# One row order for every chunk of a pointwise convolution, and its first load on a second queue

## Chip, cores and metric

The kernel runs on one core of a Trainium2 chip. The metric is device time in microseconds (us) of one execution; the profiled span is about 1.7 us shorter than that time. A run told with a profile has one execution in the trace, and its other executions only as times; a traced execution is called a look.

## The reference, cut to what matters

With `k = 1` the depthwise part is a scale of each of the 384 channels, and the rest is a matmul by the 384 x 384 pointwise weights:

```python
out = x * dw[0, 0]                                # x: 1 x 384 x 384 x 384, bf16
return jnp.einsum('bhwc,cd->bhwd', out, pw)       # pw: 384 x 384
```

That is 147456 rows of 768 bytes in, and as many out.

## The kernel before

The scale is folded into the weights at the start: the row `dw` becomes a selection matrix `sel_w`, and 18 small matmuls (L216) spread and scale the weights into `w_r`. Then come 288 supertiles of 512 rows. For each, VectorE transposes x into `T`, TensorE does 48 matmuls (L166) of 32 rows by 384 columns, four at a time in the four row groups of the array, and ScalarE casts the result from PSUM into `O`. Supertiles are loaded and stored in chunks of `L`: 1, 1, 2, 2, 4 at the start, then tens, then 6, 4, 3, 2, 1, 1, 1. The parts that the change touches:

```python
LONG = 3
...
def load_x(t):
    g, i, off, first, L = chunks[t]
    dst = Xs[g % NR][:, 4 * off : 4 * (off + L), :]
    rows = xf[512 * first : 512 * (first + L), :]
    if first + LONG < NS:                     # all chunks but the last three
        src = rows.rearrange("(p s) c -> p (s c)", p=P)
        dst = dst.rearrange("p s c -> p (s c)")
    else:                                     # the last three, one supertile each
        src = rows.rearrange("(a k q) c -> q a k c", k=4, q=4)
    ...
    nc.sync.dma_start(dst, src).then_inc(s_x[g % NR][i], 16)

def store(t):
    ...
    if first + LONG < NS:
        dst = rows.rearrange("(q p j) d -> p q (j d)", q=4, p=P)
        src = src.rearrange("p (q e) -> p q e", q=4)
    else:
        dst = rows.rearrange("(m q) d -> m (q d)", q=4)
    ...                                       # wait for the casts of the chunk
    nc.sync.dma_start(dst, src).then_inc(s_o[g % NR], 16)

nc.scalar.dma_start(dw_row[:], ...)           # depthwise row, ScalarE's queue
nc.sync.dma_start(pw_n[:], ...)               # weights, SyncE's queue
# then load_x(0), load_x(1), ... on SyncE's queue
```

For a chunk of one supertile the two branches are mirror images. "By quadrant" loads 128 pieces of 3 KB and stores 512 pieces of 768 bytes. "The other row order" loads 512 pieces of 768 bytes and stores 128 pieces of 3 KB. Load and store have to use the same one, or rows come out permuted.

## Time and profile before

| | before |
|---|---|
| time, median of 3 (range) | 575.43 us (575.23 to 576.05) |
| span of the profiled run | 573.7 us |
| TensorE, main matmuls | 561.8 us |
| head: start of the main loop | 7.18 us |
| last cast ends | 569.97 us |
| last store: issue to landing | 2.3 us |

TensorE is busy for 99% of the span. Only what stands before the first main matmul (the head) and what follows the last one (the tail) can change the time. The lines that carry this are in the prediction. One more, because the experiments turn on it, is ScalarE's timeline at the start of the main loop (start, length, engine and line, work, idle time before it and its releaser):

```profile
9.36 1.44 ACT L307 CAST O<-ps 128x1536 bf16<-128x1536 f32 x1 [0.92 <-PE ps L166]
```

This is the cast of the first supertile. It starts 9.36 - 7.18 = 2.18 us after the main loop does.

### The profile page before, as it was taken

The numbers are of one execution on the slowest core, as the hardware profiler recorded it, in microseconds if no ns is written. First come the engines' busy times: TensorE is split into PE (matmuls) and PEld (weight loads), VectorE is DVE, ScalarE is ACT, GpSimd is POOL, SyncE is SP. The second block draws the span as 40 slices with busy tenths as digits, with TensorE's granted clock in tenths as the row PEclk, the third lists the DMA queues.
The fourth block names the chain that finished last, engine by engine and source line by source line (L and its number), as shares of the span: only waits on it lengthen the run. The fifth ranks groups of instructions, "written<-read, shape, count | busy, mean of one in ns | idle before, by whom it ended". The sixth has DMA issues, their size and how long they took to land.

```text
span 573.7 us, 29706 instructions
## 1 busy us (share of the span) xinstructions
PE 567.3 (99%) x13869; PEld 414.9 (72%) x13869; DVE 509.3 (89%) x583; ACT 418.8 (73%) x296; POOL 0.9 (0%) x8
## 2 busy tenths in 40 slices
PE   8999999999999999999999999999999999999996
PEld 5777777777777777777777777777777777777774
DVE  6899999999999999999999999999999999999994
ACT  6777777777777777777777777777777777777775
POOL 0000000000000000000000000000000000000000
PEclk9999999999999999999999999999999999999999
DMA  8999999999999999999999999999999999994996
GB/s 324 432 409 417 430 397 430 444 424 422 399 408 416 384 397 436 398 383 395 432 398 384 395 429 390 393 401 429 402 385 419 401 390 397 425 394 149 402 408 251
DMA packets 25912, 226.88 MB, mean 395 GB/s; under 512 B 1197, under 2 KB 5678, under 8 KB 22062
## 3 DMA queue, kind: packets, MB, share of 16 engines
q1 hardware_dynamic: 25900, 226.79, 98.0%
q14 instruction: 9, 0.07, 0.0%
q8 instruction: 1, 0.02, 0.0%
q10 hardware_dynamic: 2, 0.00, 0.0%
HBM read 113.54 MB, written 113.25 MB: 395 GB/s over the span
## 4 chain that ended last, share of the span: by engine, by line
PE 98%; DMA 1%; ACT 0%; DVE 0%; issue 0%; SPq 0%
PE ps L166 97%; DMA pw_n<-in_pw_dram 1%; PE ps L216 1%; DMA out_dram<-O 0%; ACT O L307 0%; DVE O L304 0%; SPq L337 0%; SPq L100 0%
## 5 line engine op out<-in xcount | busy, mean ns | idle before, releaser
L166 PE MATMUL ps<-w_r,T 32*128 32x384 bf16 x13824 | 561.8, 321 | 0.1
L258 DVE STREAM_TRANSPOSE T<-X 128x384 uint32<-128x384 uint32 x576 | 506.2, 882 | 54.0 <-DMA X<-in_x_dram 2.4
L307 ACT CAST O<-ps 128x1536 bf16<-128x1536 f32 x288 | 413.5, 1436 | 147.9 <-PE ps L166 147.9
L166 PEld LDWEIGHTS ps<-w_r,T 32*128 32x128 bf16 x13824 | 412.9, 93 | 149.2 <-issue 0.7
L271 ACT CAST w_r<-ps 128x768 bf16<-128x768 f32 x5 | 3.7, 805 | 1.7 <-PE ps L216 1.6
L183 PE MATMUL ps<-zero 32*128 32x384 bf16 x24 | 2.6, 494 | 1.4 <-POOL zero L232 1.4
L304 DVE CAST O<-ps 128x768 bf16<-128x768 f32 x1 | 1.0, 958 | 3.0 <-DMA out_dram<-O 3.0
L216 PE MATMUL ps<-pw_n,sel_w 64*128 64x384 bf16 x18 | 3.0, 510 | 0.1
L183 PEld LDWEIGHTS ps<-zero 32*128 32x128 bf16 x24 | 0.7, 100 | 2.6 <-issue 2.6
L216 PEld LDWEIGHTS ps<-pw_n,sel_w 64*128 64x128 bf16 x18 | 1.2, 138 | 1.6 <-issue 1.2
L244 ACT ACT_TABLE_LOAD x1 | 1.3, 1283 | 1.5 <-SPq L100 1.5
L276 DVE TENSOR_REDUCE sel<-eye 128x64 f32<-128x128 bf16 x1 | 0.3, 290 | 1.8 <-POOL eye L234 1.8
L271 DVE CAST w_r<-ps 128x768 bf16<-128x768 f32 x1 | 1.0, 956 | 1.0 <-PE ps L216 1.0
L286 DVE TENSOR_SCALAR sel_w<-sel,dw_f 128x256 bf16<-128x256 f32 x3 | 0.9, 348 | 0.0
L283 DVE COPY dw_f<-ps 128x3 f32<-128x3 f32 x1 | 0.2, 161 | 0.8 <-PE ps L198 0.8
L198 PEld LDWEIGHTS ps<-ones,dw_row 1*128 1x128 bf16 x3 | 0.2, 98 | 0.2 <-issue 0.2
L244 ACT COPY warm<-warm 128x1 f32<-128x1 f32 x2 | 0.3, 188 | 0.0
L234 POOL TENSOR_SCALAR_AFFINE_SELECT eye<-ones 128x128 bf16<-128x128 bf16 x1 | 0.3, 292 | 0.1
L232 POOL MEMSET zero<- 128x192 uint32 x1 | 0.3, 258 | 0.0
L198 PE MATMUL ps<-ones,dw_row 1*128 1x1 bf16 x3 | 0.2, 159 | 0.0
L233 POOL MEMSET ones<- 128x128 bf16 x1 | 0.2, 204 | 0.0
L231 POOL MEMSET warm<- 128x3 f32 x1 | 0.1, 101 | 0.5 <-SPq L100 0.5
(4 smaller groups left out, 0.4 us busy)
## 6 DMA issues: line engine op xcount, KB each, us to landing
X<-in_x_dram SPq DMA_DIRECT2D x26, 3840.0 KB, 21.5
out_dram<-O SPq DMA_DIRECT2D x26, 3840.0 KB, 27.5
X<-in_x_dram SPq DMA_DIRECT2D x2, 1536.0 KB, 17.4
out_dram<-O SPq DMA_DIRECT2D x2, 1536.0 KB, 13.7
X<-in_x_dram SPq DMA_DIRECT2D x3, 768.0 KB, 8.8
out_dram<-O SPq DMA_DIRECT2D x3, 768.0 KB, 8.9
X<-in_x_dram SPq DMA_DIRECT2D x1, 2304.0 KB, 18.9
out_dram<-O SPq DMA_DIRECT2D x1, 2304.0 KB, 12.1
```

The costliest lines, as they stand in the source:

```text
L166: mm = nc.tensor.matmul(PS[s][:, q, :D], lhsT=Ts[s][32 * q : 32 * q + 32, b, par::2], rhs=w_r[32 * q : 32 * q + 32, b, par, :], start=(b, ...
L183: nc.tensor.matmul(PS[0][:, i, :D], lhsT=zero[32 * i : 32 * i + 32, 0:P], rhs=zero[32 * i : 32 * i + 32, :], start=True, stop=True, tile_p ...
L198: mm = nc.tensor.matmul(PS[1][:, 0, D + k : D + k + 1], lhsT=dw_row[:, P * k : P * k + P], rhs=ones[0:1, 0:1], start=True, stop=True,)
L216: mm = nc.tensor.matmul(PS[(k + 1) % 2][:, 2 * r + v, :D], lhsT=sel_w[64 * v : 64 * v + 64, k, r, :, :].rearrange("p q w -> p (q w)"), rhs ...
L232: nc.gpsimd.memset(zero[:].bitcast(U32), 0).then_inc(s_zero)
L234: nc.gpsimd.affine_select(out=eye[:], in_=ones[:], pattern=[[-1, P]], compare_op=mybir.AluOpType.is_equal, fill=0.0, base=0, channel_multi ...
L244: c = nc.scalar.copy(warm[:, s + 1 : s + 2], warm[:, 0:1])
L258: ins = nc.vector.transpose(out=Tw[:, 3 * h : 3 * h + 3], in_=Xw[:, :, j, 96 * h : 96 * h + 96].rearrange("p k (b w) -> p b k w", w=32),)
L271: o = nc.vector.tensor_copy(out, in_) if e == 0 else nc.scalar.copy(out, in_)
L286: nc.vector.tensor_scalar_mul(sel_w[:, k], sel[:].unsqueeze(2).to_broadcast([P, 2, 4, 32]), dw_f[:, k : k + 1]).then_inc(s_sw)
L304: e = nc.vector.tensor_copy(Ov[:, nq:4, j, :], PS[s][:, nq:4, :D])
L307: a = nc.scalar.copy(Ov[:, 0:nq, j, :], PS[s][:, 0:nq, :D])
```

## The change

Intent: one row order for all chunks, so that the special case goes away, and the first chunk of x is issued on ScalarE's queue, in parallel with the weights on SyncE's. The diff, without blank lines and context:

```diff
-LONG = 3
-        def load_x(t):
+        def load_x(t, eng=nc.sync):
-            if first + LONG < NS:
-                src = rows.rearrange("(p s) c -> p (s c)", p=P)
-                dst = dst.rearrange("p s c -> p (s c)")
-            else:
-                src = rows.rearrange("(a k q) c -> q a k c", k=4, q=4)
+            src = rows.rearrange("(p s) c -> p (s c)", p=P)
+            dst = dst.rearrange("p s c -> p (s c)")
-            nc.sync.dma_start(dst, src).then_inc(s_x[g % NR][i], 16)
+            eng.dma_start(dst, src).then_inc(s_x[g % NR][i], 16)
...
-            if first + LONG < NS:
-                dst = rows.rearrange("(q p j) d -> p q (j d)", q=4, p=P)
-                src = src.rearrange("p (q e) -> p q e", q=4)
-            else:
-                dst = rows.rearrange("(m q) d -> m (q d)", q=4)
+            dst = rows.rearrange("(q p j) d -> p q (j d)", q=4, p=P)
+            src = src.rearrange("p (q e) -> p q e", q=4)
...
         nc.scalar.dma_start(dw_row[:], ...)
+        load_x(0, nc.scalar)
         nc.sync.dma_start(pw_n[:], ...)
...
-            todo.append((g_end[g - NR] if g >= NR else -1, load_x, t))
+            if t > 0:
+                todo.append((g_end[g - NR] if g >= NR else -1, load_x, t))
```

## The prediction

> **What bounds the kernel now.** I read the page's busy shares first, then the groups of instructions, then the chain of work that ended last with windows on the first 14 us and the last 9 us, and last the timelines there.
>
> ```profile
> PE 567.3 (99%) x13869; PEld 414.9 (72%) x13869; DVE 509.3 (89%) x583; ACT 418.8 (73%) x296; POOL 0.9 (0%) x8
> ...
> PE 98%; DMA 1%; ACT 0%; DVE 0%; issue 0%; SPq 0%
> ...
> L166 PE MATMUL ps<-w_r,T 32*128 32x384 bf16 x13824 | 561.8, 321 | 0.1
> ```
>
> The matmul of the main loop is busy for 561.8 of the 573.7 us span, and in all 13824 instructions it has 0.1 us of idle time before it. 288 supertiles at 561.8 / 288 = 1.95 us each are a wall: no load, transpose, cast or store between the first and the last of them can shorten the kernel, and they lengthen it only if they make TensorE wait. What is left is 573.7 - 561.8 = 11.9 us: the head up to the first main matmul, and the tail after the last. The change touches only these and the three last chunks. The chain in the first 14 us:
>
> ```profile
> 1.01 3.03 DMA pw_n<-in_pw_dram
> 4.05 0.05 issue
> 4.09 2.96 PE ps L216 x18
> 7.05 0.12 issue
> 7.18 6.84 PE ps L166 x162
> ```
>
> The columns are start, length and what. The head of 7.18 us hangs on the load of the pointwise weights: issued at 1.01, landed at 4.05, then 18 matmuls that scale and spread the weights, then the main loop. The first chunk of x is not in it, as the timeline of this stretch shows (start, length, engine and line, work, idle before it and its releaser):
>
> ```profile
> 0.97 0.49 ACTq L131 DMA_DIRECT2D dw_row<-in_dw_dram  x1
> 1.01 0.45 SPq L132 DMA_DIRECT2D pw_n<-in_pw_dram  x1
> 1.49 1.28 ACT L244 ACT_TABLE_LOAD   x1 [1.49 <-SPq L100]
> 1.52 3.49 SPq L113 DMA_DIRECT2D X<-in_x_dram  x7
> 4.63 3.80 ACT L271 CAST w_r<-ps 128x768 bf16<-128x768 f32 x5 [1.56 <-PE ps L216]
> 4.96 0.96 DVE L271 CAST w_r<-ps 128x768 bf16<-128x768 f32 x1 [1.00 <-PE ps L216]
> 5.83 1.55 DVE L258 STREAM_TRANSPOSE T<-X 128x384 uint32<-128x384 uint32 x2
> 8.00 1.57 DVE L258 STREAM_TRANSPOSE T<-X 128x384 uint32<-128x384 uint32 x2 [0.62 <-DMA X<-in_x_dram]
> ```
>
> The first pair of transposes has no idle time before it: VectorE came from its weight cast, and the first chunk (issued 1.52, fastest landing of the seven loads 3.5 us, so 5.0) was there already. The second pair waits 0.62 us for the second chunk, but its first half is ready at 8.8, and TensorE needs it at 7.18 + 1.95 = 9.13. So neither load sets the head. At the other end, the queue of SyncE:
>
> ```profile
> SPq L141 <- DMA out_dram<-O: 2.0, 1, 2.0
> SPq L127 <- DVE O L304: 1.1, 1, 1.1
> ```
>
> The last cast ends at 569.97, the last store is issued at 570.1, and SyncE then waits 2.0 us for it to land (2.3 us from issue). That is about 572.4, and some 1.3 us of closing semaphore work end the span. Here a store is exposed in full.
>
> **What the Trainium skill says.** (1) "DMA: Bandwidth & Descriptors", section "Bandwidth", says small HBM descriptors pay a fixed overhead each, and its table of rules says to coalesce. The trace agrees: its packet records last 36 ns (median) at 768 B, 67 ns at 1536 B, 96 ns at 2304 B and 124 ns at 3072 B, which is about 10 ns plus 37 ns per KB. (2) The same page, "Issuing engines are not separate DMA queues": loads issued from two engines run on the same 16 DMA engines and interleave, and a second issuer only saves sequencer time; its section on queues adds that each engine goes round the rows packet by packet. The trace before cannot confirm this for large loads, as ScalarE issues only one 768 B row; the new profile will. (3) "TensorE: Matmul & The Clock Gate", Part 1: the array runs at half rate until it has been busy for one window of about 3.4 us, and the window is free-running. The trace agrees on the two rates: the 18 spreading matmuls go in pairs 0.32 us apart, the main loop in fours 0.16 us apart, both with 384 columns; the fast rate begins at 7.18.
>
> **Part by part.** First, the load of the first chunk goes to ScalarE. Removed: one issue of about 0.5 us on SyncE, so the second chunk is issued at about 1.5 instead of 2.0. Added: one issue of about 0.5 us on ScalarE between its row of depthwise weights and its table load. The table load moves from 1.49 to about 2.0, the two copies after it end at 3.07 + 0.5 = 3.6; the weight casts start at 4.63. So 1.0 us of slack swallows 0.5 us: zero on the path. The first chunk itself is issued at 0.97 + 0.49 = 1.46, against 1.52: it gains nothing as an issue. But it no longer stands behind the weights. Before, on one queue, the weights' 384 packets of 768 B started at about 2.4 and had all started by 4.0, with the chunk's 128 packets of 3072 B filling in behind. Now both queues are served at once. Packets follow an issue by about 1.4 us here, so the chunk starts near 2.85. At that time roughly 98 of the weights' 384 packets are through. What is then to be moved is 286 x 36 ns / 16 = 0.64 us of weights and 128 x 121 ns / 16 = 0.97 us of x. Served in turn, one packet each, the 8 large packets per engine all go before the weights' 18 small ones are done, so the weights end at 2.85 + 1.61 = 4.46 if the engines are full, against about 3.9: later by 0.55 us. The weights before did not fill the engines in that stretch (38 to 62 packets in 0.2 us against 83 at best), so this is an estimate that may be 0.3 too high or, if the large packets win more turns, 0.4 too low. The spreading matmuls, casts and the main loop all move with the landing: **+0.55 us on the path**. The first chunk lands earlier than 5.0, worth zero since VectorE is busy until 5.9 (and then later still).
>
> Second, the three last loads take 3 KB a partition in one run instead of four rows of 768 B: 128 packets for 512 in each. Their packets run near 519 us in the trace, some 40 us before their use, and TensorE waits 0.1 us in all. Saved: 3 x (512 x 36 - 128 x 124) ns / 16 = 0.5 us of DMA time in a stretch where it is hidden: zero.
>
> Third, the three last stores (384 KB each) go out by quadrant: 512 pieces of 768 B instead of 128 of 3072 B. Per store: 512 x 38.6 / 16 = 1.24 us (by the line fitted above) against 128 x 124 / 16 = 0.99 us: +0.25 us. The first of the three queues behind the chunk before, the second runs from 569.6 to 570.8 and the last starts at 571.2, so 0.25 us more in the second does not reach the last; only the last counts: **+0.25 us**. ScalarE's last casts, VectorE's half and the issue length (0.33 to 0.37 us, the same for 128 and 512 pieces) don't change.
>
> Fourth, a knock-on of the first part: TensorE's filler matmuls end at 4.02 and the next start on the landing of the weights. 0.07 us of idle time becomes about 0.6. If the clock window that made the array fast at 7.18 is then not busy enough, or if the loop starts before it as often as after it, part of the first supertiles runs at half rate: up to one window of 3.4 us at half speed, 1.7 us. I give this one chance in four, about **+0.35 us** on average.
>
> Sum: 0.55 + 0.25 + 0.35 = 1.15 us on 575.43 = 576.6; the middle of the outcomes lies a little below the mean, so I predict 576.4.
>
> **Rivals.** (a) Head unchanged or better: the two rings don't delay the weights, because the weights' slow ramp (38 to 40 packets per 0.2 us) shows that descriptor supply and not the engines limits them, and x fills gaps. Then the weights land at 4.05 still and the time is 575.43 + 0.25 = 575.7. For it: the ramp. Against it: from 3.2 on the engines were full. (b) The clock gate flips a window later: 0.55 + 0.25 + 1.4 to 1.7 gives 577.6 to 577.9. For it: the flip in the profile coincides with the start of the loop, so there is no margin to lose. Against it: the window from 3.8 to 7.2 would still be some 80% busy. (c) The tail pays more, if 768 B writes to memory ramp as slowly as the weights' reads did (1.5 us for 384 packets, so 2.0 for 512, against 1.0): +1.0 at the tail, 577.1 in all. Against it: the 512-piece store of 1536 B ran at 67 ns a piece from its first 0.2 us on. (d) Faster: a second chunk issued 0.5 us sooner. It would need a wait of TensorE for it, and there is none.
>
> **Range and chances.** The three timed runs spread over 575.23 to 576.05, so 0.4 us either way is noise. Rival (a) sets the low end, 575.3; (b) the high end, 577.9. 2% is 11.5 us; everything the change touches, head and tail, is 11.9 us, so faster by 2% is out of reach, and slower by 2% needs a stall in the main loop of which I find no cause: within 2% 98%, slower 1%, faster 1%.
>
> **What would show it.** Right: the chain begins with the weights' load of about 3.6 us instead of 3.03; the first main matmul starts near 7.7; the second chunk lands sooner; the last store takes 2.5 to 2.6 us to land instead of 2.3; the main loop stays at 561.8 us. Wrong: the weights land at 4.05 as before, or the first chunk becomes what the main loop waits for, or the three last supertiles make TensorE wait, or the span grows in the middle.

## The result

The changed kernel takes 576.16 us (median of 6, 575.92 to 576.47), the kernel before 575.47 us (median of 6 beside it, 575.14 to 576.05). The ratio is 1.0011, 95% interval 0.9998 to 1.0024. A ratio here is the mean time of one kernel's fast runs over that of the other's fast runs of the same rounds, so it isn't quite the ratio of the medians. The medians differ by 0.69 us; the interval just includes no difference at all. Both are far inside 2%.

The changed kernel's profile (the main matmul is now L160, the spreading L210). The busy shares and the main group first:

```profile
PE 567.5 (99%) x13869; PEld 386.1 (67%) x13869; DVE 507.6 (88%) x583; ACT 418.9 (73%) x296; POOL 0.9 (0%) x8
...
L160 PE MATMUL ps<-w_r,T 32*128 32x384 bf16 x13824 | 561.9, 321 | 0.0
```

The wall is the same: 561.9 us, with no idle time before the main matmuls. Next the chain in the first 14 us (start, length, what):

```profile
1.02 3.11 DMA pw_n<-in_pw_dram
4.13 0.05 issue
4.18 3.06 PE ps L210 x17
7.24 0.03 issue
7.27 6.76 PE ps L160 x138
```

The weights land at 4.13, not at the 4.6 that was forecast, and the loop starts at 7.27 against 7.18. The timeline of the head:

```profile
1.53 0.37 ACTq L108 DMA_DIRECT2D X<-in_x_dram  x1
1.92 1.28 ACT L238 ACT_TABLE_LOAD   x1 [1.92 <-issue]
4.72 3.80 ACT L265 CAST w_r<-ps 128x768 bf16<-128x768 f32 x5 [1.22 <-PE ps L210]
5.92 8.40 DVE L252 STREAM_TRANSPOSE T<-X 128x384 uint32<-128x384 uint32 x10
9.55 1.44 ACT L301 CAST O<-ps 128x1536 bf16<-128x1536 f32 x1 [1.02 <-PE ps L160]
```

The table load came 0.43 us later and cost nothing: ScalarE still waits 1.22 us for the first spread weights. The transposes run without a gap there. The first main cast starts 9.55 - 7.27 = 2.28 us after the loop, 0.10 more than before. At the other end, SyncE's waits:

```profile
SPq L135 <- DMA out_dram<-O: 2.4, 1, 2.4
SPq L119 <- DVE O L298: 1.1, 1, 1.1
```

SyncE waits 2.4 us for the last store, against 2.0; that store lands 2.8 us after its issue, against 2.3. Between the two kernels the span grew by 0.7 us. By the lines above, 0.09 of it is the later start of the loop, 0.10 is inside the first supertile, and about 0.4 to 0.5 is the last store. The experiments ask which of these belong to the change and which are chance.

The rate view of the DMA engines, from 570 to 575 us in slices of 0.125 us, shows the last stores. The kernel before, then the changed one:

```profile
GB/s 418 393 295 49 0 0 0 344 393 393 393 393 418 393 369 50 0 0 0 0 0 0 0 0 0 0 0 0 0 0 0 0 0 0 0 0 0 0 0 0
```

```profile
GB/s 344 313 332 326 313 332 240 49 12 201 313 313 326 319 326 319 332 344 295 105 25 0 0 0 0 0 0 0 0 0 0 0 0 0 0 0 0 0 0 0
```

Both rows end with the last store, and the group ahead of it is the store before. With 3 KB pieces the engines move 393 GB/s, and there is an empty pause of three slices between the two stores. With 768 bytes they move about 320 GB/s, and there is no empty slice between the stores any more.

### The profile page after: what moved, and what is told of

Read it like the earlier page. It is cut to its first block, busy times and chain, and to the rows that moved or that the text cites. A ratio compares the mean times of both kernels' runs of the same rounds, so it can differ in the third digit from the quotient of the medians.

```text
span 574.4 us, 29706 instructions
## 1 busy us (share of the span) xinstructions
PE 567.5 (99%) x13869; PEld 386.1 (67%) x13869; DVE 507.6 (88%) x583; ACT 418.9 (73%) x296; POOL 0.9 (0%) x8
## 4 chain that ended last, share of the span: by engine, by line
PE 98%; DMA 1%; DVE 0%; issue 0%; SPq 0%
PE ps L160 98%; DMA pw_n<-in_pw_dram 1%; PE ps L210 1%; DVE O L298 0%; SPq L331 0%; SPq L98 0%
## 5 line engine op out<-in xcount | busy, mean ns | idle before, releaser
L160 PE MATMUL ps<-w_r,T 32*128 32x384 bf16 x13824 | 561.9, 321 | 0.0
L160 PEld LDWEIGHTS ps<-w_r,T 32*128 32x128 bf16 x13824 | 384.1, 93 | 178.1 <-issue 0.7
L210 PE MATMUL ps<-pw_n,sel_w 64*128 64x384 bf16 x18 | 3.1, 521 | 0.2 <-DMA pw_n<-in_pw_dram 0.2
L210 PEld LDWEIGHTS ps<-pw_n,sel_w 64*128 64x128 bf16 x18 | 1.2, 139 | 1.8 <-issue 1.2
## 6 DMA issues: line engine op xcount, KB each, us to landing
out_dram<-O SPq DMA_DIRECT2D x3, 768.0 KB, 10.7
```

The costliest lines, as they stand in the source:

```text
L160: mm = nc.tensor.matmul(PS[s][:, q, :D], lhsT=Ts[s][32 * q : 32 * q + 32, b, par::2], rhs=w_r[32 * q : 32 * q + 32, b, par, :], start=(b, ...
L210: mm = nc.tensor.matmul(PS[(k + 1) % 2][:, 2 * r + v, :D], lhsT=sel_w[64 * v : 64 * v + 64, k, r, :, :].rearrange("p q w -> p (q w)"), rhs ...
```

## The experiments

All are single edits of the kernel before, unless said otherwise. The times of "before" for a group of runs are those of the same chip.

### e1: the head alone

```diff
+        load_x(0, nc.scalar)          # after the depthwise row; the rest of the head as in the change
```

> Only the first load of x goes to ScalarE's queue; the last three chunks as before. Theory (the 0.7 us is two costs, head 0.1 and tail 0.5, plus up to 0.2 from where the clock's step falls): the weights land at 4.1 to 4.2 against 4.05, main loop starts at 7.2 to 7.3, last store lands in 2.3 us, median 575.5 to 575.8. Rival (the head carries it all, the tail's transfer is hidden): last store 2.3 us but median 576.1 or more. Rival of the prediction (weights delayed by the interleaved chunk): weights at 4.6, main loop at 7.7.

Measured: 575.3, 575.56, 576.62, 576.72 and 577.42 us (median 576.62; ratio 1.0017, interval 1.0003 to 1.0031), before 575.54 (575.16 to 575.86). The profiled execution, 575.56, has weights at 3.96, loop at 7.09, last store in 2.4 us. So the median spoke for the rival and the trace for the theory, and the scatter of 2.1 us was new. The two further looks (f, below) return to this.

### e2: the tail alone

```diff
-LONG = 3
+LONG = 0
```

> Only the last three chunks change (3 KB loads, stores by quadrant); first load of x stays on SyncE's queue. Theory: head as before (weights land 4.05, loop at 7.2), last store lands in 2.8 us against 2.3, SyncE's wait for it 2.4 to 2.5 against 2.0, median 575.9 to 576.1. Rival (the tail costs what the packet law says, 0.25): last store 2.55 us, median 575.7. Rival (all is chance of the clock's step): no difference to before.

Measured: 576.40 us (575.99 to 576.59, 5 runs) against 575.54; ratio 1.0016, interval 1.0002 to 1.0029. SyncE's wait for the last store:

```profile
SPq L141 <- DMA out_dram<-O: 2.6, 1, 2.6
```

The last store lands in 3.0 us. All five runs are above all nine of the kernel before. The tail alone therefore gives at least the whole difference (0.86 against 0.69), more than the 0.25 us that its packets should cost. It changes two things, though, the three loads and the three stores; e3 and e4 take it apart.

### e3: only the very last chunk

```diff
-            if first + LONG < NS:
+            if first + LONG < NS or first + 1 == NS:      # in load and in store
```

> Only the very last chunk is loaded in 3 KB and stored by quadrant; the two before it keep the old order. Theory (only the last store is exposed): last store lands in 2.8 us and the time is that of the whole tail change, 575.9 to 576.1. Rival (the stores before it crowd it): last store nearer 2.5 us, time halfway.

Measured: 575.66 us (575.64 to 576.01, 4 runs), before 575.63 (575.14 to 577.11); ratio 0.9999, interval 0.9985 to 1.0014. In the profile the last store takes 2.6 us. In time the theory missed; in the trace the store lies between 2.3 and the 2.8 to 3.0 of the whole tail change, as the rival said: **what stands ahead of the last store matters too**. The two stores ahead of it and two of the three loads kept the old form here, so this run doesn't tell which of them it is; e4 does. The packet records show the size. A store ends with 16 small writes to its semaphore, one from each engine. The table below gives for each look when the 16th of the second-last store lies, against the first packet of the last store.

### e4: the loads alone, and what a late engine looks like

```diff
-            if first + LONG < NS:
+            if True:                                      # in the load only: rows permuted on purpose
```

> Only the three last loads change to 3 KB a partition, the stores keep the old row order: rows of the last 1536 come out permuted, a wrong result on purpose. Theory: the loads are hidden, so TensorE has no idle time in the main loop, last store 2.3 us, time within 0.3 us of before. Rival (the loads' form also matters, by what they displace): some idle time of TensorE in the last three supertiles or the main loop longer than 561.9 us.

Measured: 576.77 us, one run, wrong result as intended. The main matmuls:

```profile
L166 PE MATMUL ps<-w_r,T 32*128 32x384 bf16 x13824 | 562.2, 321 | 0.0
```

They have no idle time: the loads' form is hidden from TensorE. (The busy time is 0.3 us above the 561.9 named, which is the clock, below.) Yet the time isn't within 0.3 us. The first cast and the rate view from 570 us (slices of 0.125 us) show why:

```profile
9.64 1.44 ACT L307 CAST O<-ps 128x1536 bf16<-128x1536 f32 x1 [1.31 <-PE ps L166]
```

```profile
GB/s 393 393 393 418 393 74 66 0 0 246 393 369 418 418 393 393 393 123 25 25 25 25 25 25 25 25 0 0 0 0 0 0 0 0 0 0 0 0 0 0
```

First, the cast starts 9.64 - 7.08 = 2.56 us after the loop, 0.38 more than before. Second, the last store runs at 393 GB/s as before, and then for eight slices at 25 GB/s, which is a sixteenth of 393. One DMA engine of the sixteen is a microsecond late, and the store lands in 3.4 us. The cast's delay has nothing to do with the loads, as the unchanged kernel shows it too (f, below). The late engine has. SyncE's timeline from 511 to 537 us shows the issues of the last five loads of x and of the two stores behind them, in the kernel before and in e4:

```profile
511.42 14.91 SPq L113 DMA_DIRECT2D X<-in_x_dram  x5
526.38 9.38 SPq L128 DMA_DIRECT2D out_dram<-O  x2
```

```profile
511.71 2.32 SPq L113 DMA_DIRECT2D X<-in_x_dram  x5
516.15 19.89 SPq L128 DMA_DIRECT2D out_dram<-O  x2
```

In the kernel before, the store behind the loads is issued 10 us later. There a load in the other row order ends with four semaphore writes where one by quadrant ends with sixteen (1196 such writes in the whole trace, 1232 in e4: 3 x 12 more), so only four engines carry it: from 520 to 530 us the sixteen engines together move 96 GB/s, against 393 in e4. That long stretch has a use. In all fourteen looks one engine has fallen 5.5 to 10.7 us behind the other fifteen by the store that lands from 513 us on. At a store of 540 to 544 us the last engine is only 0.3 to 1.2 us behind the one before it, in all ten looks with at least two old loads: the late engine has caught up while the four worked. With three new loads it is still 7.0 to 8.2 us behind at 546 us, in all four looks (this one, e2 and both of the changed kernel), and 1.8 to 2.9 at a store issued near 561 us, two ahead of the last three. So the loads' rival was right, though by another way than idle time of TensorE: the new form takes away a stretch in which most DMA engines had little to do. Why that one engine falls behind, no run here shows.

### e7: a dose of small pieces

```diff
+            if je + 1 == NS:          # last store in 1024 pieces of 384 B, columns wrong on purpose
+                src = Os[g % NR][:, (4 * off - 4) * D : 4 * (off + L) * D]
+                src = src.rearrange("p (n r e) -> p n r e", n=8, r=2)[:, :, 0, :]
+                dst = dst.rearrange("m (n e) -> m n e", n=8)
```

> The kernel before, with only the last store cut into 1024 pieces of 384 B (columns wrong on purpose). A dose of the suspected cost. Theory A (time per piece, about 10 ns plus 37 ns per KB on each of 16 engines): 64 pieces x 24 ns = 1.54 us of packets against 0.99, so landing in about 2.9 us. Theory B (a further cost of many pieces besides the packets, 0.25 us for 512, growing with their number): landing 3.3 us or more. If pieces under 512 B are penalised for themselves: over 4 us.

Measured: 577.86 us, one run; last store in 4.5 us. Its rate view from 570 us:

```profile
GB/s 406 418 406 393 393 148 49 90 25 49 25 49 49 194 237 224 230 246 233 224 240 224 233 224 237 218 218 166 22 22 22 18 18 15 0 0 0 0 0 0
DMA packets 1178, 0.75 MB, mean 149 GB/s; under 512 B 1060, under 2 KB 1070, under 8 KB 1177
```

The plateau is at 230 GB/s; the packets last 26 ns, against 24 by the fitted line, so 64 x 26 = 1.66 us per engine. The law of the packets holds. There are two things besides. The issue takes 0.64 us against 0.33, and the first packet starts 1.39 us after the cast ends against 0.93, so Theory B is right too: many pieces also start late. The rest is again one or two engines at 25 to 49 GB/s, late from the stores before. By its landing alone the run would speak for the third answer (over 4 us); the packets say that it is the late engines that take it there.

### e5: the first chunk ahead of everything on ScalarE's queue

```diff
+        load_x(0, nc.scalar)
         nc.scalar.dma_start(dw_row[:], ...)
```

> The first chunk of x is ScalarE's first issue, ahead of the depthwise row, so it is issued at about 1.0 beside the weights on SyncE, not 0.5 us after; tail as before. Theory A (the queues are served in turn; in the changed kernel x came too late to interleave): now weights and x share the engines from the start and the weights land 0.4 to 1.0 us later than 4.05; main loop at 7.6 to 8.2, median 576.0 to 576.6. Theory B (descriptors of one request are made before those of the next, so the earlier issue alone decides): weights land at 4.05 to 4.2 if SyncE is first, about 5 if ScalarE is.

Measured: 577.98 us (577.83 to 578.38, 4 runs), before 575.63; ratio 1.0040, interval 1.0025 to 1.0054. The chain:

```profile
0.97 0.43 ACTq L113
1.40 0.03 issue
1.43 3.47 DMA dw_row<-in_dw_dram
```

The chain now runs through the 768 bytes of the depthwise row, which stands behind 384 KB of x on the same queue and lands at 4.90. I had not foreseen that, so as a test of the weights the time says little. The packet records still answer the question about turns. The weights' first packet starts at 2.98, when 75 of the chunk's 128 packets had started, though the two were issued within 0.05 us. The weights land at 4.8, which fits either theory. The order of the packets is Theory B as far as it goes: the request that is second by a little gets no turn until the first is more than half through.

### e6: the weights behind the first chunk

```diff
+        load_x(0)                     # SyncE, ahead of the weights
         nc.sync.dma_start(pw_n[:], ...)
```

> On SyncE's queue the first chunk of x is issued before the weights; tail as before. The dose of a late landing of the weights. Theory (the head hangs on the weights' landing alone): weights land about 0.5 us (issue) plus up to 1.0 us (transfer of x) later, at 4.6 to 5.5, and the main loop starts later by exactly as much. The time grows by the same amount to within 0.5 us, the rest being where the clock's step falls. Rival (the depthwise row, the scaling and casts set the head): main loop starts within 0.2 us of 7.18.

Measured: 577.34 us (576.26 to 578.66, 4 runs), ratio 1.0030, interval 1.0012 to 1.0048. The chain:

```profile
1.47 3.45 DMA pw_n<-in_pw_dram
4.92 0.05 issue
4.97 3.06 PE ps L218 x18
8.03 0.03 issue
8.06 6.03 PE ps L168 x112
```

The weights land 0.87 us later than before (4.92 against 4.05), and the loop starts 0.88 us later (8.06 against 7.18). The head does hang on that landing, one for one. The span grew by 1.5 us, so another 0.6 went elsewhere: the first cast starts at 10.90, 2.84 us after the loop and not 2.18. The median of the four runs grew by 1.7 us, more than the 0.9 with 0.5 either way that was expected; the three runs without a trace are not explained.

### e8: a try at beating both

```diff
-        nc.sync.dma_start(pw_n[:], ...)
+        for k, eng in enumerate((nc.sync, nc.scalar, nc.sync)):
+            eng.dma_start(pw_n[:, k, :], pw[P * k : P * k + P, :]).then_inc(s_pw[k], 16)
+        load_x(0, nc.scalar)
...
+            nc.tensor.wait_ge(s_pw[k], 16)        # one wait for each third
```

> A try at beating both: the weights in three loads of 96 KB (thirds 1 and 3 on SyncE, 2 on ScalarE), each with its own semaphore, the first chunk of x behind on ScalarE, tail as before. If the weights' landing sets the head: the first third lands near 3.5, the spreading matmuls begin up to 0.5 us sooner, main loop at 6.7 to 6.9, median 575.0. If the depthwise row or the casts then set it, or the clock's step now falls inside the loop: 575.4, no gain.

Measured: 576.33 us (575.66 to 579.35, 6 runs), ratio 1.0016, interval 0.9997 to 1.0036: no gain. The traced execution is a slow one of the six (577.76). The spreading matmuls did start at 3.95, but x became the wait, as VectorE's timeline shows:

```profile
6.74 1.56 DVE L261 STREAM_TRANSPOSE T<-X 128x384 uint32<-128x384 uint32 x2 [0.97 <-DMA X<-in_x_dram]
```

The first chunk, issued 0.4 us later than in the changed kernel and sharing the engines with the second chunk on the other queue, lands only at 6.7; TensorE waits 1.5 us and the loop starts at 7.70. The last store has late engines again, 4.1 us, here with the old loads: several engines are up to 2.3 us behind near 566 us.

### f: before, after and the head alone, looked at again on one chip

No edit but those already shown.

> The kernel before, looked at a second time, beside the looks that follow on the same chip. If the scatter of 575.1 to 577.1 comes from where the clock's step falls and from one DMA engine that is late with the last store, this look shows both in its sizes: span = 573.7, plus half of what the step lies after the start of the main loop, plus what the last store takes over 2.3 us, to within 0.2 us.

> The changed kernel, looked at a second time. If the tail's cost belongs to the change, the last store again takes 2.6 to 3.0 us (2.3 to 2.4 with 3 KB pieces where no engine is late) and its first 90% of packets end 1.1 to 1.2 us after the first starts, against 1.0. If it was chance, 2.3 to 2.4.

> The head change alone again, to see what its slow runs are (575.3 to 577.4 in five). If the head change makes them: the first chunk, now sharing the engines with the second, lands after 5.9 us, and the transposes or the main loop wait for it, or the weights land past 4.2. If chance makes them: weights at 4.1 and no wait for x, and what is over 575.5 lies in the clock's step and in the last store.

> The same kernel once more, for the same question and with the same two answers.

Measured: before 575.79, after 576.54, the head alone 575.69 and 575.34 us. The sum expected of the kernel before, 573.7 plus half of the clock's step inside the loop, gives 574.1, and the span is 574.1. These are the first casts of before and after in this pair:

```profile
9.74 1.44 ACT L307 CAST O<-ps 128x1536 bf16<-128x1536 f32 x1 [1.25 <-PE ps L166]
```

```profile
9.05 1.44 ACT L301 CAST O<-ps 128x1536 bf16<-128x1536 f32 x1 [0.92 <-PE ps L160]
```

Here the head of the changed kernel is 0.69 us the faster, where it was 0.19 the slower in the first pair. And this is the changed kernel's last store, in SyncE's wait and in the rate view from 570 us:

```profile
SPq L135 <- DMA out_dram<-O: 3.4, 1, 3.4
```

```profile
GB/s 332 338 240 49 18 154 332 326 338 319 332 338 379 307 283 111 12 12 25 25 18 25 25 25 6 0 0 0 0 0 0 0 0 0 0 0 0 0 0 0
```

It takes 3.7 us: 325 GB/s as expected, then one engine that is a microsecond late.

### All looks side by side

All times count from the start of the span. The step is the moment at which the trace's clock record goes to full rate. "Late" is the 16th semaphore write of the last store less the 15th. "Overlap" is the 16th write of the second-last store less the first packet of the last one: positive means that the last store starts while an engine still works on the one before. All in us.

| look | weights land | loop starts | clock step | loop to first cast | cast end to first packet | first packet to 90% done | overlap | late | last store lands in |
|---|---|---|---|---|---|---|---|---|---|
| before | 4.05 | 7.18 | 6.82 | 2.18 | 0.93 | 1.00 | -0.28 | 0.03 | 2.3 |
| before, again | 4.09 | 7.22 | 7.95 | 2.52 | 0.93 | 1.00 | -0.40 | 0.03 | 2.3 |
| e1, head alone | 3.96 | 7.09 | 7.37 | 2.30 | 0.93 | 1.01 | -0.27 | 0.10 | 2.4 |
| head alone, again | 4.06 | 7.19 | 7.53 | 2.33 | 0.93 | 1.01 | -0.27 | 0.09 | 2.4 |
| head alone, third | 4.03 | 6.97 | 5.02 | 2.18 | 0.93 | 1.01 | -0.27 | 0.10 | 2.4 |
| e4, loads alone | 3.94 | 7.08 | 7.91 | 2.56 | 0.99 | 1.01 | 0.91 | 0.95 | 3.4 |
| after | 4.13 | 7.27 | 7.51 | 2.28 | 1.01 | 1.18 | 0.00 | 0.14 | 2.8 |
| after, again | 3.93 | 6.87 | 5.26 | 2.18 | 1.11 | 1.13 | 0.82 | 1.06 | 3.7 |
| e2, tail alone | 3.87 | 7.04 | 6.00 | 2.18 | 1.08 | 1.11 | 0.57 | 0.37 | 3.0 |
| e3, last alone | 4.01 | 7.15 | 6.96 | 2.18 | 1.01 | 1.15 | -0.07 | 0.02 | 2.6 |

Three terms are enough for the span: the loop's start, half of what the clock's step lies inside the loop, and the landing time of the last store. In all fourteen looks the span less these three is 564.17 to 564.24 us. Of the 0.70 us between the first two profiles they give 0.09, 0.12 and 0.50. Three things follow.

**The head.** The weights land between 3.93 and 4.13 in the five looks with the chunk on ScalarE's queue, and between 3.87 and 4.09 in the five without. The head part of the change costs nothing that these looks can see.

**The clock's step.** Where the step comes before the loop, the first cast follows the loop by 2.18 us. Where it comes after, the delay is 2.18 plus half of what the step lies inside the loop, to 0.04 us: a half of 0.37 (before, again) gives 2.55 for a measured 2.52, one of 0.42 (e4) gives 2.60 for 2.56, and e6 with a step at 9.46 in a loop from 8.06 gives 2.88 for 2.84. The kernel before has it at 6.82 once and at 7.95 once, so it isn't the kernel that places it. The Trainium skill ("TensorE: Matmul & The Clock Gate", Part 1) calls the clock's window free-running and 3413 ns long. The looks agree: the step lay at 4.79 to 9.46 us, and in twelve of the fourteen looks full rate lasted 566.61 us, 166 such windows (165 and 167 in the others).

**The tail.** It has two costs, and they come from different halves of the edit. The small pieces: with 768 bytes the last store's first packet comes 0.08 us later and 90% of it takes 0.10 to 0.18 us longer; without a late engine (e3) that makes 2.6 for 2.3. (In the looks with overlap the first packet comes up to 0.18 us later, but with 3 KB pieces too, 0.06 in e4.) The late engine, up to 1.1 us on top: it comes with the loads (e4), and is carried over where the last store starts while that engine still works on the one before. The 768-byte stores didn't make it, as it was late before they were issued. They only shorten the pause ahead of the last store that the other fifteen engines have, from 0.4 to 0.2 us. The stores alone, with the old loads, were not run.

## Why the prediction was right or wrong

The measured 576.16 lies in the range 575.3 to 577.9 and 0.24 from the 576.4 named; "within 2%" was right. The sum came out nearly right from terms that were not, so its closeness is luck.

- **"+0.55 us on the path" for the moved load: failed.** The weights landed 0.08 later in the first look and not later at all over five. Two things were wrong in that step. I had placed the packet records some 0.3 us wrong against the instruction times, so "roughly 98 of the weights' 384 packets" through was too few: when the chunk's first packet started, at 3.00, it was 205, and in the other four looks 228 to 316. And "served in turn, one packet each" doesn't describe what followed: in the next 0.6 us, 175 of the weights' packets started and 32 of the chunk's. e5 shows the late first turn with the roles changed. The Trainium skill ("DMA: Bandwidth & Descriptors", "Queues, rings and completion order"), on which I had leaned, has each engine go round its queues at packet granularity, and a packet there is a group, typically of 9 to 17 descriptors; I took each packet record of the trace for a turn. Between two loads in full swing the trace does show turns (the chunk's and the second chunk's packets mixed from 3.8 to 4.8), but the request that was issued first was more than half through before the other got its first. That first turn came after 13 to 20 of the weights' 24 pieces per engine, on average, which fits turns of many pieces better than turns of one; where a turn ends, the trace doesn't mark. So rival (a) was right for the head.
- **That the head hangs on the weights' landing: right.** e6 delayed it by 0.87 us and the loop by 0.88 us.
- **Zero for the table load and for the second chunk's earlier issue: right.** The first chunk "lands earlier than 5.0": wrong, in the changed kernel it landed at 5.5 (1.53 + 3.9), while the second landed at 6.1 instead of 8.0. VectorE was free at 5.92, so this cost nothing here; e8, which issued it a little later still, shows how near that wait was.
- **Zero for the loads of the last chunks: failed.** TensorE indeed had 0.0 us of idle time in e4 and after. But the sum of the saved DMA time divided by 16 engines, where the old loads ran on four, and what ran "near 519 us" was the start of a stretch at 96 GB/s in which a late engine caught up. The new loads took that stretch away, and the engine was still up to 1.06 us late with the last store, in the four looks that have them.
- **"+0.25 us" for the last stores: right for their pieces.** The packets last 39 ns as the line said (38.6), and the last store alone (e3) took 0.3 us longer, of which 0.08 was a later first packet. That "0.25 us more in the second does not reach the last" held for fifteen engines, which were done with it 0.2 us before the last one's first packet in the changed kernel. It failed for the late one: in the changed kernel it ended the second-last store with the last one's first packet at 571.16, and in e2 and the second look at the changed kernel 0.57 and 0.82 us after it. The last store took 2.6 to 3.7 us in four looks, against 2.3 to 2.4 where no engine was late with 3 KB.
- **"+0.35 us" for the clock: right as a mechanism, wrong as a cost of the change.** Half of the time that the step lies inside the loop is lost, 0.1 us in the profiled run. But the step moves from run to run, and the kernel before pays it as well. In its first look the step was at 6.82, not with the loop at 7.18 as I had read it.

With the head at zero and the clock at chance, the +0.69 is the tail's: e2, the tail alone, gives +0.86, and the head alone gives nothing in its three looks. Within the tail the split is read from traces: about 0.3 for the stores' pieces and up to 1.1 for the engine that the loads leave late; e4's single run, loads alone, was 1.2 us above the kernel before, and e3's showed no difference in time. Two points stay open. Late engines of over 0.3 us also reach the last store in two of the nine looks with three old loads (e7 and e8), where it is several engines and not one. And the three slow runs of e1 (576.6 to 577.4), which give it as large a mean difference as e2's, were in no trace: the two further looks at that kernel fell in good runs. The seven runs of the changed kernel, which has the same head, stayed below 576.6, so I don't put those down to the head, but haven't shown what they were.

No version here beats the kernel before.

## What to carry to other kernels

Where one engine is busy for 98% of the span, look only at its first and last instruction: what stands before the first can be checked by delaying it on purpose, as e6 did, and what follows the last counts in full, so the last transfer should have few, large pieces, and a pause ahead of it in which a late engine can catch up. A transfer for which no compute engine waits may still matter: ask what it makes the transfers behind it do. Before a difference below 1 us is explained, look at the same kernel twice: here the clock's step alone moved the unchanged kernel by 0.34 us. And several small losses that add up to the measured sum are no proof of any one of them.

## What the Trainium skill lacked or had wrong

- "DMA: Bandwidth & Descriptors", "Specifications", puts line rate at 512 bytes and up. Here stores of 384 KB moved 393 GB/s in 3 KB pieces, about 320 in 768-byte pieces and 230 in 384-byte pieces.
- The same page, "Latency and other measured facts", gives about 600 ns to the first byte for loads and stores from SyncE. Here the first packet of the last store started 0.83 us after the issue began, and its delay after the cast grew with the number of pieces: 0.93 us for 128 and 1.01 for 512 without overlap, 1.39 for 1024 (with overlap). The page has no such growth; the issue itself took 0.33, 0.37 and 0.64 us.
- The same page, "Queues, rings and completion order", gives turns of whole packets, typically 9 to 17 descriptors, but no number for loads like these. Of two requests on two queues issued 0.04 to 0.5 us apart, the second got its first packet record only when 53% to 82% of the first one's had started (205 to 316 of 384 in five looks; 75 of 128 in e5), which is 13 to 20 of 24, or 5 of 8, for each engine. Why, no run here shows.
- The same page names two engines that are usually slower and ties that, as a best guess, to transfers issued from GpSimd. Here all large transfers came from SyncE and ScalarE, and one engine was 5.5 to 10.7 us behind the other fifteen by the store at 513 us in all fourteen looks, and in five of them the last engine ended the last store 0.37 to 1.06 us after the one before it; the trace doesn't say which engine it was.
